# Eight row-split dk stores in place of five in a one-core attention forward and backward kernel

## The chip, the core and the metric

The kernel runs on one core of a Trainium2 chip. The core has a matrix engine (TensorE, PE in the profile), a vector engine (VectorE, DVE), a scalar engine (ScalarE, ACT), a general engine (GpSimd, POOL) and a queue engine (SyncE, SP). Transfers between HBM and the on-chip memory (SBUF) are issued by SP, ACT or POOL and carried out by 16 DMA engines that all issuers share. The metric is the device time of one execution in microseconds, lower is better. The kernel before took 1267.52 us (median of three runs, 1266.84 to 1269.59).

## The reference

A decode attention with its gradients, for 2 x 32 = 64 heads, one query row per head, 8192 keys of 128 numbers, all in bf16:

```
scores = einsum("bhqd,bhkd->bhqk", q, k) * D**-0.5      # Sq = 1, Sk = 8192, D = 128
p      = softmax(scores)
out    = einsum("bhqk,bhkd->bhqd", p, v)
out, vjp = jax.vjp(forward, q, k, v);  dq, dk, dv = vjp(grad_out)
returns out, dq, dk, dv
```

The inputs k and v are 2 MiB per head each, and so are the outputs dk and dv: dv is the outer product of p and grad_out, dk that of the score gradient and q. Everything else is small. So the kernel reads 268 MB and writes 268 MB.

## The kernel before, in words

**Tiles.** A head's k is one SBUF tile of 128 partitions x 64 x 128 bf16: partition p holds 64 consecutive keys, 16 KB that also lie together in HBM. v is the same. There are 12 such tiles (`NTILE`), so six heads are in flight. dk and dv are written over k and v in place: `outer` (line 469) multiplies on VectorE a quarter of a tile at a time, and after the fourth quarter it issues the store of the whole tile. A "row" below is one partition's 16 KB of a store or load: a load or a whole-tile store is 128 rows.

**Stages.** The loop at line 506 takes one step per quarter tile, eight steps per head (four quarters of k, then four of v), and overlaps four heads. Each step transposes a quarter on TensorE (`transpose_chunk`, line 232), copies it out of PSUM on ScalarE (line 241, two PSUM buffers), forms scores of the previous quarter (`score_chunk`), and does softmax, sums and outer products of earlier heads. The order on every engine is the order of the text (`pin`).

**Queues.** Loads go out on SP (`load`, line 106). The load of head i+6 reuses the tile of head i, so SP waits until that tile's store has landed everywhere. Whole-tile stores go out on POOL (line 493); those of the last head go out on SP in quarters. Every DMA is signalled by a semaphore; SP and ACT issues share one set of eight in rotation, POOL has another eight. A new DMA on a semaphore first waits for the landing of the previous one on it.

**The special stores.** `SPREAD` (line 23) names heads 6, 17, 28, 39 and 50. Their dk is not stored as 128 rows in one DMA, but by `by_rows` (line 96) in four: rows 8 to 127 (120 rows) with a cap on the descriptor (`cut`), then rows 0-2, 3-5 and 6-7 without. `turn(0)` (line 88) puts POOL's choice of DMA engine back to its start; `turn(n)` moves it on by issuing a tiny copy of n rows of 16 bytes into a scratch tile. `BACK` (line 26) asks, five steps after each special store, for `turn(0)` and `turn(5)`. At the start, five rows of q are loaded in the same way (line 129), which brings the choice to 5 for the first special store. The other 59 rows of q and the 64 rows of grad_out are loaded by SP (line 135).

Of the kernel before, what the change touches and what calls it, by code (L numbers as in the profile page):

```python
# [19 lines left out]
SW = 32  # L20
NTILE = 12
FIRST = 5
SPREAD = {
    i: ((8, 128, True), (0, 3, False), (3, 6, False), (6, 8, False)) for i in range(6, 56, 11)
}
BACK = {i + 1: FIRST for i in SPREAD}

@with_exitstack
def kernel(  # L30
# [11 lines left out]
    nc = tc.nc  # L42
    B, H, Sq, D = q.shape
# [5 lines left out]
    NT = Sk // P  # L49
# [6 lines left out]
    store_eng = nc.gpsimd  # L56
    pin = tc.keep_in_program_order
# [30 lines left out]
    def turn(n):  # L88

        if n:  # L90
            parts = turns.pop()
            pin(store_eng.dma_start(out=parts[:n, :], in_=q_rows[:n, : 2 * QT], max_dma_last_dim=2 * QT))
        else:
            pin(store_eng.inc_swdge_sem([], [], mode="reset_dge_cursor"))

    def by_rows(dst, src, steps):

        for step in steps:
            if len(step) == 1:
                turn(*step)  # L100
                continue
            p0, p1, cut = step
            cap = {"max_dma_last_dim": NT * D} if cut else {}
            pin(store_eng.dma_start(out=dst[p0:p1], in_=src[p0:p1], **cap))

    def load(i, w, pieces=(NCH,)):
        h = heads[i]
        t = kvp.tile([P, NT, D], BF16, tag=f"kv{slot_of(i, w)}", name="kvt")
        h.tile[w] = t
        src = (v_v if w else k_v)[i]  # L110
        c = 0
        for m in pieces:
            n0, n1 = c * CH, (c + m) * CH
            pin(load_eng.dma_start(out=t[:, n0:n1, :], in_=src[:, n0:n1, :]))
            c += m
# [1 line left out]
    load(0, 0, (1, 1, 2))  # L117

    q_rows = q.rearrange("b h s d -> (b h s) d")
    NTURN = len(BACK) + sum(len(step) == 1 and step[0] > 0 for x in SPREAD.values() for step in x)  # L120
    parts_all = const.tile([CH, NTURN, 2 * QT], BF16, name="parts_all")
    turns = [parts_all[:, n, :] for n in range(NTURN)]

    qd_nat = evp.tile([P, CH, P], BF16, tag="ev", name="qd_nat")
    for w, a in enumerate((q, grad_out)):
        rows = a.rearrange("b h s d -> (b h s) d")
        r0 = FIRST if w == 0 else 0
        if r0:
# [3 lines left out]
                    out=qd_nat[:r0, w, :], in_=rows[:r0], max_dma_last_dim=D  # L132
# [28 lines left out]
    for g in range(SG):  # L161
        nc.vector.tensor_copy(
            out=sel4[g * SW : (g + 1) * SW, :, g // 2, :],
            in_=ident_f[g * SW : (g + 1) * SW, g * SW : g * SW + 2 * NCH].rearrange(
                "p (c t) -> p c t", t=2
            ),
# [9 lines left out]
    for w in range(2):  # L176
        nc.vector.tensor_copy(
            out=qd_pair[:BH, w],
            in_=qd_nat[:BH, w, :]
# [33 lines left out]
    def window(i, w):  # L213

        pin(nc.scalar.copy(out=qwin[:, w, :, Q0 : Q0 + 2], in_=qpair[:, w, i]))
# [253 lines left out]
    def outer(i, w, c, ends):  # L469

        h = heads[i]
        n0 = c * CH
        shape = [P, CH, D // 2, 2]
        pin(
            nc.vector.tensor_tensor(  # L475
                out=h.tile[w][:, n0 : n0 + CH, :].rearrange("p n (e t) -> p n e t", t=2),
                in0=h.qb[w][:]
                .rearrange("p (e t) -> p e t", t=2)
                .unsqueeze(1)
                .to_broadcast(shape),  # L480
                in1=h.pair[w][:, n0 : n0 + CH, :].unsqueeze(2).to_broadcast(shape),
                op=ALU.mult,
            )
        )
        if c + 1 in ends:
            at = ends.index(c + 1)
            b0, b1 = (ends[at - 1] if at else 0) * CH, (c + 1) * CH
            dst = (dv_v if w else dk_v)[i]
            if w == 0 and i in SPREAD:
                by_rows(dst, h.tile[w], SPREAD[i])  # L490
            else:
                eng = load_eng if len(ends) > 1 else store_eng
                pin(eng.dma_start(out=dst[:, b0:b1, :], in_=h.tile[w][:, b0:b1, :]))  # L493
# [12 lines left out]
    for g in range(SL * BH + O0 + NCH + 4 - SL):  # L506
        now = [(g // SL - b, g % SL + b * SL) for b in range(4)]
        now = [(i, r) for i, r in now if 0 <= i < BH]

        def at(r0):  # L510

            return next((i for i, r in now if r == r0), None)

        def within(r0):

            return next(((i, r - r0) for i, r in now if r0 <= r < r0 + NCH), None)

        if (i := at(O1 + NCH)) is not None and i + AHEAD < BH:
            load(i + AHEAD, 0)
        if (i := at(O0 + NCH)) is not None and i + AHEAD < BH:  # L520
            load(i + AHEAD, 1)
        if x := within(O1):
            outer(x[0], 1, x[1], last if x[0] == BH - 1 else whole)
        if (i := at(O1 + NCH)) in BACK:
            turn(0)
            turn(BACK[i])
        if x := within(O0):
            outer(x[0], 0, x[1], last if x[0] == BH - 1 else whole)
        ev = None
        if g < SL * BH:  # L530
            i, r = divmod(g, SL)
            if r == NCH:
                begin(i)
                broadcast(i, 1)
            if r == NCH + 2:
                broadcast(i, 0)
            ev = transpose_chunk(i, r)
        if (i := at(A1 + NCH + 2)) is not None:
            join(i, 1)
        if (i := at(A0 + NCH + 2)) is not None:  # L540
            join(i, 0)
        if x := within(A1):
            acc(x[0], 1, x[1])
        if x := within(A0):
            acc(x[0], 0, x[1])
        if (i := at(NCH + 1)) is not None:
            spread_rows(i, 0)
        if (i := at(SL + 1)) is not None:
            spread_rows(i, 1)
        if (i := at(NCH + 3)) is not None:  # L550
            max_spread(i)
            expo(i)
        if prev is not None:
            score_chunk(*prev)
        prev = (g // SL, g % SL, ev) if ev is not None else None
        if (i := at(NCH + 1)) is not None and i + 1 < BH:
            window(i + 1, 0)
        if (i := at(1)) is not None and i > 0:
            window(i, 1)

        if (i := at(NCH)) is not None:
            keep_raw(i)
        if (i := at(SL)) is not None:
            keep_raw(i)
        if (i := at(NCH + 1)) is not None:
            max_part(i)
        if (i := at(NCH + 2)) is not None:
            max_all(i)
        if (i := at(NCH + 4)) is not None:
            normalise_p(i)  # L570
        if (i := at(SL + 1)) is not None:
            weigh(i)
        if (i := at(SL + 2)) is not None:
            normalise_ds(i)
        if (i := at(A1 + NCH)) is not None:
            pick(i, 1)
        if (i := at(A0 + NCH)) is not None:
            pick(i, 0)
# [37 lines left out]
```

## Time and profile before

| what | value |
|---|---|
| time, median of three runs | 1267.52 us (1266.84 to 1269.59) |
| the profiled execution's own time | 1267.85 us |
| its span, first to last instruction | 1266.1 us |
| TensorE busy | 1187.7 us, 94% |
| VectorE, ScalarE, GpSimd busy | 1031.3, 557.2, 80.6 us |
| bytes read from and written to HBM | 268.47 and 268.47 MB, 424 GB/s over the span |
| granted TensorE clock, mean | 0.988 |

The page gives for each engine the busy time, then 40 equal slices of the span in which each digit is a busy share in tenths. The line DMA is the mean busy share of the 16 DMA engines. "Issue to landing" is the time from a DMA's issue until its last part has arrived. The trace also holds one record per DMA packet (start, length, queue, bytes), but no number of the DMA engine that moved it. Queue q0 is POOL's, q1 is SP's; q8 and q14 carry the engines' instructions. All times inside the run are counted from the span's start.

### The profile page before, as it was taken

To read this page: it belongs to the slowest core of one execution; us is meant where nothing else is said; L and a number is where in the kernel's file an instruction comes from. 1 tells how busy PE (TensorE), PEld (TensorE's weight loads), DVE (VectorE), ACT (ScalarE), POOL (GpSimd) and SP (SyncE) were. 2 spreads that over 40 slices of the span, in tenths; PEclk is the share of its full clock that TensorE was granted. 3 is DMA by queue.
4 is the path that set the end of the run, shared out by engine and by line. 5 is a ranking of instruction groups with operands and counts; after the bars stand their busy time and mean duration, and the time that the engine had idled before them with its cause. 6 is when DMAs were issued, how large, how long until landed. Compare 5 with 4: busy or idle time off the path is not lost.

```text
span 1266.1 us, 24581 instructions
## 1 busy us (share of the span) xinstructions
PE 1187.7 (94%) x10056; PEld 783.1 (62%) x10056; DVE 1031.3 (81%) x2267; ACT 557.2 (44%) x769; POOL 80.6 (6%) x153
## 2 busy tenths in 40 slices
PE   6999999999999999999999999999999999999981
PEld 4666666666666666666666666666666666666650
DVE  3888888888888888888888888888888888887883
ACT  3444444444444444444444444444444444444430
POOL 0000010000010000001000001000000001000000
PEclk9999999999999999999999999999999999999995
DMA  9999999999999999999999999999999999999998
GB/s 393 422 429 429 429 428 429 429 429 429 430 429 428 429 429 429 429 429 429 423 428 430 430 429 428 428 427 430 429 430 428 429 429 427 429 429 429 429 430 336
DMA packets 39741, 538.53 MB, mean 425 GB/s; under 512 B 5236, under 2 KB 5236, under 8 KB 6516
## 3 DMA queue, kind: packets, MB, share of 16 engines
q1 hardware_dynamic: 20172, 272.70, 50.6%
q0 software_dynamic: 19456, 264.25, 49.1%
q8 instruction: 79, 1.29, 0.4%
q14 instruction: 34, 0.28, 0.1%
HBM read 268.47 MB, written 268.47 MB: 424 GB/s over the span
## 4 chain that ended last, share of the span: by engine, by line
PE 68%; DVE 16%; DMA 7%; another core or an unknown queue 4%; issue 2%; ACT 0%; SPq 0%; POOL 0%; ACTq 0%; DVEq 0%
PE tp L239 29%; PE acc L420 17%; PE raw L260 11%; DVE kvt L475 6%; PE sw L280 4%; DMA out_dram<-kvt 4%; DVE sel L443 4%; DVE rows L273 3%; DMA kvt<-in_v_dram 3%; PE sw L366 3%; PE sw L221 2%; PE sw L304 1%; DVE sel L437 1%; PE acc L457 1%
## 5 line engine op out<-in xcount | busy, mean ns | idle before, releaser
L241 ACT COPY ev<-tp 128x1024 f32<-128x1024 f32 x512 | 518.7, 1013 | 660.3 <-PE tp L239 654.8
L475 DVE TENSOR_TENSOR kvt<-qb,pair 128x2048 bf16<-128x2048 bf16 x512 | 617.2, 1216 | 0.2
L239 PE MATMUL tp<-ident_f,kvt 128*128 128x128 f32 x4096 | 547.6, 277 | 3.1 <-DMA kvt<-in_v_dram 2.6
L239 PEld LDWEIGHTS tp<-ident_f,kvt 128*128 128x128 f32 x4096 | 454.0, 144 | 84.2 <-issue 64.6
L260 PE MATMUL raw<-ev,qwin 128*32 128x512 bf16 x2048 | 209.5, 399 | 0.0
L420 PE MATMUL acc<-kvt,dS_pad 128*64 128x512 bf16 x1024 | 160.7, 395 | 0.8 <-DVE dS_pad L406 0.8
L420 PE MATMUL acc<-kvt,E_pad 128*64 128x512 bf16 x1024 | 159.5, 391 | 0.6 <-DVE E_pad L331 0.6
L280 PEld LDWEIGHTS sw<-sel,rows 128*128 128x128 f32 x1024 | 123.9, 191 | 52.4 <-DVE sel L443 25.9
L443 DVE SCALAR_TENSOR_TENSOR sel<-acc,diag,sel 128x128 f32<-128x128 f32 x384 | 134.7, 351 | 13.6
L260 PEld LDWEIGHTS <-qwin 128*32 128x32 bf16 x2048 | 52.7, 93 | 135.4 <-issue 131.0
L280 PE MATMUL sw<-sel,rows 128*128 128x16 f32 x1024 | 136.3, 265 | 0.0
L493 POOL DMA_DIRECT2D out_dram<-kvt x121 | 64.6, 533 | 1062.3 <-DVE kvt L475 484.4
L273 DVE COPY rows<-raw 128x512 f32<-128x512 f32 x128 | 88.6, 692 | 47.0 <-PE raw L260 47.0
L299 DVE TENSOR_REDUCE st<-sw 1x1 f32<-1x128 f32 x64 | 17.8, 278 | 55.9 <-PE sw L298 55.9
L221 PE MATMUL sw<-ident_f,qT 128*128 128x128 bf16 x128 | 28.9, 226 | 36.2 <-DVE st L294 36.2
L420 PEld LDWEIGHTS <-dS_pad 128*64 128x64 bf16 x1024 | 36.6, 108 | 34.9 <-issue 31.8
L366 PEld LDWEIGHTS sw<-st,ones 128*128 128x128 f32 x256 | 37.9, 186 | 31.0 <-issue 15.3
L420 PEld LDWEIGHTS <-E_pad 128*64 128x64 bf16 x1024 | 36.0, 108 | 33.6 <-issue 31.5
L366 PE MATMUL sw<-st,ones 128*128 128x1 f32 x256 | 48.8, 260 | 0.5 <-DVE st L337 0.5
L437 DVE TENSOR_SCALAR sel<-acc,diag 128x128 f32<-128x128 f32 x128 | 43.8, 342 | 0.0
L457 PEld LDWEIGHTS acc<-ones,sel 128*128 128x128 f32 x256 | 39.0, 193 | 7.2 <-DVE sel L443 7.2
L457 PE MATMUL acc<-ones,sel 128*128 128x1 f32 x256 | 36.7, 212 | 6.1 <-DVE sel L443 6.1
(54 smaller groups left out, 381.3 us busy)
## 6 DMA issues: line engine op xcount, KB each, us to landing
out_dram<-kvt POOLq DMA_DIRECT2D x121, 2048.0 KB, 44.9
kvt<-in_v_dram SPq DMA_DIRECT2D x64, 2048.0 KB, 20.1
kvt<-in_k_dram SPq DMA_DIRECT2D x63, 2048.0 KB, 20.2
out_dram<-kvt POOLq DMA_DIRECT2D x5, 1920.0 KB, 49.5
out_dram<-kvt SPq DMA_DIRECT2D x8, 512.0 KB, 20.1
kvt<-in_k_dram SPq DMA_DIRECT2D x2, 512.0 KB, 4.4
kvt<-in_k_dram SPq DMA_DIRECT2D x1, 1024.0 KB, 6.9
out_dram<-kvt POOLq DMA_DIRECT2D x10, 48.0 KB, 49.1
```

The source lines that it names most:

```text
L239: pin(nc.tensor.transpose(tp[:, m, :], two, ident_f[:]))
L241: pin(nc.scalar.copy(out=ev[:], in_=tp[:]))
L260: nc.tensor.matmul(h.raw[g * SW : (g + 1) * SW, :], lhsT=qwin[:, w, e, q0 : q0 + SW], rhs=cols[:, b, :, e], start=(c == 0), stop=(c == NCH ...
L273: pin(nc.vector.tensor_copy(out=h.rows[:], in_=h.raw[:]))
L280: nc.tensor.matmul(h.score[w].rearrange("p (n m t) -> p n m t", m=QT, t=2)[:, :, m, :], lhsT=h.rows[:, m * P : (m + 1) * P], rhs=sel4[:].r ...
L366: nc.tensor.matmul(out, lhsT=ones[:].to_broadcast([P, P]), rhs=col, start=True, stop=True)
L420: nc.tensor.matmul(h.acc[w][g : g + CW, :], lhsT=wts[:, n0 : n0 + CW], rhs=rows[:, n0 : n0 + QT, :].rearrange("p n d -> p (n d)"), start=( ...
L437: nc.vector.tensor_scalar(out=h.sel[:], in0=block, scalar1=diag[:, 0:1], scalar2=None, op0=ALU.mult)
L443: nc.vector.scalar_tensor_tensor(out=h.sel[:], in0=block, scalar=diag[:, b : b + 1], in1=h.sel[:], op0=ALU.mult, op1=ALU.add,)
L457: nc.tensor.matmul(h.acc[w][:, 0:1], lhsT=h.sel[:], rhs=ones[:], start=True, stop=True)
L475: nc.vector.tensor_tensor(out=h.tile[w][:, n0 : n0 + CH, :].rearrange("p n (e t) -> p n e t", t=2), in0=h.qb[w][:] .rearrange("p (e t) -> ...
L493: pin(eng.dma_start(out=dst[:, b0:b1, :], in_=h.tile[w][:, b0:b1, :]))
```

## The change

Eight heads instead of five have a special dk store. At heads 6, 15, 24 and 32 it is the same split as before (120 rows, then 3, 3 and 2). At heads 40, 47, 51 and 55 the large piece has 104 rows; at 40 the other 24 rows follow in one piece, at 47, 51 and 55 a piece of 17 capped rows after a `turn` of 11 or 15, and a last piece of 7 rows. The pieces without the cap (the small rows) are no longer issued by POOL: `by_rows` keeps them in a list, and ScalarE issues them at the start of the next step. `BACK` now holds the turns for each head: reset and 5 after the first three, and 2, 12, 4 and 14 without a reset after the next four.

```diff
+SMALL = ((0, 3, False), (3, 6, False), (6, 8, False))
 SPREAD = {
-    i: ((8, 128, True), (0, 3, False), (3, 6, False), (6, 8, False)) for i in range(6, 56, 11)
+    6: ((8, 128, True),) + SMALL,
+    15: ((8, 128, True),) + SMALL,
+    24: ((8, 128, True),) + SMALL,
+    32: ((8, 128, True),) + SMALL,
+    40: ((24, 128, True), (0, 24, False)),
+    47: ((0, 104, True), (11,), (104, 121, True), (121, 128, False)),
+    51: ((0, 104, True), (15,), (104, 121, True), (121, 128, False)),
+    55: ((24, 128, True), (11,), (0, 17, True), (17, 24, False)),
 }
-BACK = {i + 1: FIRST for i in SPREAD}
+BACK = {7: (0, 5), 16: (0, 5), 25: (0, 5), 33: (2,), 41: (12,), 48: (4,), 52: (14,)}
...
+    pending = []
+
     def by_rows(dst, src, steps):
...
             p0, p1, cut = step
-            cap = {"max_dma_last_dim": NT * D} if cut else {}
-            pin(store_eng.dma_start(out=dst[p0:p1], in_=src[p0:p1], **cap))
+            if cut:
+                pin(store_eng.dma_start(out=dst[p0:p1], in_=src[p0:p1], max_dma_last_dim=NT * D))
+            else:
+                pending.append((dst[p0:p1], src[p0:p1]))
...
-    NTURN = len(BACK) + sum(len(step) == 1 and step[0] > 0 for x in SPREAD.values() for step in x)
+    NTURN = sum(n > 0 for x in BACK.values() for n in x) + sum(
+        len(step) == 1 and step[0] > 0 for x in SPREAD.values() for step in x
+    )
...
+        for dst, src in pending:
+            pin(nc.scalar.dma_start(out=dst, in_=src))
+        pending.clear()
...
         if (i := at(O1 + NCH)) in BACK:
-            turn(0)
-            turn(BACK[i])
+            for n in BACK[i]:
+                turn(n)
```

## The prediction

> **What bounds the kernel now.** I read the page from the top: engines, DMA line, queues, DMA issues. Then the busy time by stretches, SP's waits, SP's last issues, and the DMA view of the last 20 us.
>
> ```profile
> span 1266.1 us, 24581 instructions
> ...
> PE 1187.7 (94%) x10056; PEld 783.1 (62%) x10056; DVE 1031.3 (81%) x2267; ACT 557.2 (44%) x769; POOL 80.6 (6%) x153
> ...
> DMA  9999999999999999999999999999999999999998
> ...
> q1 hardware_dynamic: 20172, 272.70, 50.6%
> q0 software_dynamic: 19456, 264.25, 49.1%
> q8 instruction: 79, 1.29, 0.4%
> q14 instruction: 34, 0.28, 0.1%
> ...
> out_dram<-kvt POOLq DMA_DIRECT2D x121, 2048.0 KB, 44.9
> kvt<-in_v_dram SPq DMA_DIRECT2D x64, 2048.0 KB, 20.1
> ...
> out_dram<-kvt POOLq DMA_DIRECT2D x5, 1920.0 KB, 49.5
> ...
> out_dram<-kvt POOLq DMA_DIRECT2D x10, 48.0 KB, 49.1
> ```
>
> TensorE looks as busy as the DMA engines, but the DMA line is full from the first slice on. The stretches (us, then the four busy times, POOL's, clock, DMA share, GB/s):
>
> ```profile
> 740.00:1060.00 320.00, 310.26 (x2645) 204.90 (x2642) 269.46 (x590) 146.53 (x203) 21.38 (x39) 1.00 1.01 429
> ...
> 1220.00:1250.00 30.00, 18.18 (x124) 9.94 (x122) 23.62 (x50) 4.05 (x6) 0.54 (x2) 0.74 1.01 428
> 1250.00:1266.00 16.00, 0.00 (x0) 0.00 (x0) 0.00 (x0) 0.00 (x0) 0.00 (x0) 0.50 0.61 251
> ```
>
> The DMA share is 1.01 until 1250 us, while computing has ended by then. SP's waits and last issues, and the DMA digits from 1246 to 1266 us (0.5 us each):
>
> ```profile
> SPq L114 <- DMA out_dram<-kvt: 1124.7, 119, 27.5
> ```
>
> ```profile
> 1238.31 7.07 SPq L493 DMA_DIRECT2D out_dram<-kvt  x5
> 1247.34 3.54 SPq L585 DMA_DIRECT2D out_dram<-nat  x2
> ```
>
> ```profile
> DMA  9999999979977977978696786866666542100000
> ```
>
> SP spends 1124.7 us waiting to reload a tile whose store has not landed: loads follow stores, not computing. The last store is issued at 1250.4 us, so the last 14 us are only backlog, and the digits fall early: some DMA engines finish long before others. Hence the end is the work of the slowest of 16 engines, and what the change moves between them is all that counts.
>
> **Which engine ends when.** On a busy engine a packet starts 3 or 4 ns before the recorded end of the one before (611 ns for 16 KB, so 607 ns a row; 6 ns for a 4-byte packet). Strung together like this, the packet records of 100 to 1265 us fall into 16 chains with almost no gap. Every whole-tile DMA shows there as 8 rows and a 4-byte semaphore write. Marks name some chains: the five-row turns put a 16-byte packet on five (engines 0 to 4); one of these five gets no row of the 120-row stores (engine 4), only fillers; rows 0-2, 3-5 and 6-7 always fall on the same three of the five (engines 0, 1, 2: 3, 3, 2 rows). SP's 59 rows of q (a prime) all lie on one of these three.
>
> - engine 0: 15 extra rows over five stores; ends at 1259.4 us
> - engine 1: 15 extra rows, an 8 KB instruction fetch every 122 us (as many as ScalarE would need); 1264.5, the last
> - engine 2: 10 extra rows; 1256.8
> - engine 3: a fetch every 66 us, at 0.6 us each; 1263.8
> - engine 4: 40 rows fewer, but 628 instead of 612 ns a row; 1259.3
> - eight of engines 5 to 15: in strict rotation the 16 KB fetches of q8, 9 to 10 each, 1.33 us each; 1261.6 to 1263.2
> - the other three: no fetch, no extra row; work done by 1250.5 to 1251.3
>
> Their mean is 1259.9 (from the last stretch: 1250 + 0.61 x 16 = 1259.8), so perfect balance would save 4.6 us, 0.36%. 1.6 us pass from the last packet to the span's end and 1.75 from there to the profiled time, 1267.85, which is 0.33 above the median.
>
> **The change part by part.** *Rows.* A capped piece goes in equal shares to the largest number of engines up to 16 that divides its rows (120 rows: 15 with 8; the prime 59: one), starting where the last capped piece stopped (after 5: engine 5 on, 4 left out). So 104 rows take 13 engines, 17 one. Counting on: after head 32 the place is 4, the turn of 2 makes it 6, head 40 leaves out 3 to 5; 12 makes 15, head 47 leaves out 12 to 14, and 11 puts the 17 rows on engine 7; 4 makes 12, head 51 leaves out 9 to 11, 15 puts 17 on engine 8; 14 makes 7, head 55 leaves out 4 to 6, 11 puts 17 on 15. Uncapped rows start at engine 0: 24 give 2 each to 0-11, 7 one each to 0-6. After minus before, in rows: engines 0, 1: 17 - 15 = +2; 2: +3; 3: -3; 4: -3; 5: -11; 6: -3; 7, 8: +19; 9-11: -6; 12-14: -8; 15: +17 (sum 0).
>
> At 0.607 us a row: engine 1 gains 1.2 us; +19 is 11.5 us, which the three idle engines have; engine 3 falls to 1262.0, 9 to 14 to 1258 or 1259.
>
> *Fillers.* A left-out engine gets a 4-byte filler per packet of a taking one (16 on engine 4 per store). A 17-row piece is 34 half-row packets, so 34 x 6 ns on every other engine, three times: 0.6 us. Eleven turns instead of six: 0.1 us.
>
> *Small rows on ScalarE.* 16 issues of 0.33 us (as SP's) on an engine busy 44%; POOL loses 15 of 0.5 us, at 6% busy. Both cost nothing while the backlog lasts; without it they would sit in ScalarE's copies, for which TensorE's transposes wait. The new instructions and their waits, some 40 against a fetch of 128, bring engine 1 0 or 0.6 us of fetching; I take 0.2.
>
> *Waits added.* A small store waits for VectorE's last outer product (1.2 us) and for the previous DMA on its semaphore. In the changed order that is a load still under way: by the landings of before, ScalarE would wait at head 32 for the v of head 35 (lands 665.5, ScalarE there at 655.6): 9.9 us; at 55 7.2, at 51 5.0, at 6 3.5, at 24 3.0, at 47 1.1. Queued behind are the copies, then TensorE. Bounds for the end: 0 to 9.9 us (not their sum: each wait leaves computing later relative to loads, which shortens the next). But computing runs ahead of DMA by 0.8 us a head (a load landed 16.2 us before use at head 36, 1.8 at head 54), so before, its lead was spent by head 56. Of 9.9 us, 7 heads of 0.8 leave at most 4 at the end, which 12 us of backlog hide: 0. Without that backlog it would be 4. SP and POOL: their DMAs wait for one five to eight places back; loads land in 20.1 us and come every 9.8, so that is past; POOL's special issues wait for fewer semaphores than before (74.9 us of such waits, all hidden).
>
> *Sum.* Engine 1: 1264.5 + 1.2 + 0.7 + 0.2 = 1266.6; the next, 7 or 8: 1251.2 + 11.5 + 0.5 = 1263.2. With 1.6 + 1.75 after it: 1269.95 against 1267.85, **+2.1 us; from the median 1269.6 us**, +0.16%. A measurement of this kernel tells about 0.2% (2.5 us) from no change.
>
> [...] One chain is slow by 16 ns a row, and it is engine 4's, the one that the 120-row stores pass over; the chains of 5 to 15 run at 611 to 612 ns, fetches apart. [...]
>
> **The rivals.**
>
> 1. *The loaded engines are not the idle ones (slower).* The records do not number engines 5 to 15. For the match: the trace has eight with fetches and three without, the change takes rows from exactly eight of the eleven (5, 6, 9-14) and loads three; against: nothing else ties them. If one of 7, 8, 15 carries fetches, it ends at 1262.6 + 11.5 + 0.5 = 1274.6, time 1277.6. It decides once a loaded engine's old end is over 1255. Chance 0.13.
> 2. *The 17-row piece is shared out* (two rows each on engines 0 to 7, one on 8, as 17 = 8 x 2 + 1, if the cap is not what chooses). Engine 1 gets 6 rows more, 3.6 us, and fillers fall to nearly none: 1272.6. For: the uncapped pieces begin at 0; against: every capped piece ran in equal shares. Chance 0.08.
> 3. *ScalarE's waits become the path.* Computing would have to end over 12 us later; with the longest wait twice, 20 us, less 12: 8 us, 1275.5. Against: each shortens the next. Chance 0.05.
> 4. *Engine 1 is relieved* (ScalarE's small rows start elsewhere, or the last chain is one of the eight). Then engines 7 and 8 end last at 1263.2: -1.3 us, 1266.2. For: no ScalarE store is in the trace; against: SP's uncapped 59 rows went to one of engines 0 to 2. Chance 0.14.
>
> **How the numbers follow.** My forecast has 0.60, own range 1267.5 to 1271.0 (fetch, fillers, the spread of the runs). It is within 0.2% (up to 1270.05) for 0.37, slower for 0.22, faster for 0.01. Rival 4 adds 0.11 to the same and 0.03 to faster, rivals 1 and 2 0.21 to slower, rival 3 0.03 to slower and 0.02 to the same. So faster 0.04, same 0.50, slower 0.46. Eight in ten: from rival 4's end with the runs' spread, 1265.5, to past rival 2, 1275.0; rival 1 stays out.
>
> **What would show it.** The DMA digits of the last 16 us should fall later and more steeply, with the last packet at about 1266.6. The three early chains should end near 1262 to 1263; the last should be the one with ScalarE's fetches. At head 32 ScalarE should show a wait of several us for a load, and the loads' lead should still shrink to near 0. A chain that ends beyond 1270 alone means rival 1 or 2; a full DMA line with computing beyond 1260, rival 3. Any idle DMA time before 1240 us would make the whole sum wrong.

## The result, and the profile after

The changed kernel took 1281.31 us (median of six runs, 1279.62 to 1287.74) against 1267.65 us (six runs, 1266.84 to 1269.59) for the kernel before: a ratio of 1.0113, 95% interval 1.009 to 1.0135. That is 13.7 us slower, where 2.1 us were forecast and 1275.0 was the upper end of the range. The profiled execution took 1282.98 us.

From the page of the changed kernel: the span, the engines, three of the forty-slice rows, the queues (packets, MB, share of 16 engines) and some DMA issues.

```profile
span 1281.2 us, 24594 instructions
...
PE 1190.4 (93%) x10056; PEld 784.7 (61%) x10056; DVE 1031.6 (81%) x2267; ACT 557.3 (43%) x769; POOL 79.8 (6%) x146
...
PE   6999999999999999999969999999999999999991
...
DMA  9999999999999999999999999999999999999996
GB/s 391 424 430 430 427 430 428 429 429 428 428 428 431 429 428 430 424 428 430 427 431 424 423 431 427 425 418 427 428 424 424 412 399 411 415 410 416 428 430 282
...
q1 hardware_dynamic: 20172, 272.70, 50.0%
q0 software_dynamic: 21200, 263.00, 48.9%
q10 hardware_dynamic: 142, 1.26, 0.4%
...
out_dram<-kvt POOLq DMA_DIRECT2D x118, 2048.0 KB, 45.3
out_dram<-kvt POOLq DMA_DIRECT2D x4, 1920.0 KB, 43.2
out_dram<-kvt POOLq DMA_DIRECT2D x4, 1664.0 KB, 61.1
```

The engines' busy times are those of before within 3 us, so the work has not grown. The DMA row is as full as before. What has changed is the row under it: the DMA engines are just as busy, but in slices 32 to 37 (993 to 1185 us) they move 399 to 416 GB/s, where most slices have 424 to 431. The same by stretches:

```profile
740.00:1060.00 320.00, 310.84 (x2646) 205.22 (x2645) 269.96 (x591) 146.68 (x204) 22.81 (x39) 1.00 1.01 421
1060.00:1220.00 160.00, 151.67 (x1291) 100.26 (x1292) 131.86 (x287) 70.45 (x97) 11.53 (x20) 1.00 1.01 417
1220.00:1250.00 30.00, 27.03 (x209) 16.00 (x208) 25.41 (x58) 10.00 (x14) 1.60 (x3) 0.93 1.01 428
1250.00:1282.00 32.00, 3.73 (x16) 1.80 (x14) 8.48 (x17) 0.00 (x0) 0.00 (x0) 0.50 0.65 272
```

The last three columns are the granted clock, the DMA share and GB/s. The second of these stretches in the kernel before:

```profile
1060.00:1220.00 160.00, 152.34 (x1288) 99.96 (x1287) 131.57 (x287) 70.88 (x98) 10.62 (x20) 1.00 1.01 429
```

The same DMA share of 1.01 with 417 in place of 429 GB/s means that packets take longer; a busy engine is not an engine at its rate. ScalarE's and SP's waits, and the DMA row from 1262 to 1282 us (0.5 us a digit):

```profile
ACT ev L255 <- PE tp L253: 644.4, 503, 2.6
ACT ev L255 <- DMA out_dram<-kvt: 13.1, 1, 13.1
```

```profile
SPq L126 <- DMA out_dram<-kvt: 1136.6, 116, 27.8
```

```profile
DMA  7989988899676765553442311110000000000000
```

ScalarE stands once for long, 13.1 us at head 32. SP still spends nearly all its time waiting for stores to land. The last digits show an end that is later, and flatter than in the kernel before.

**Where the time is, packet by packet.** Strung into 16 chains as for the prediction, the packet records confirm the allotment of rows: 120 rows on 15 engines, 104 on 13, 17 on one, ScalarE's 24 on twelve and its 7 on seven. The three chains with a 17-row piece are the ones without TensorE's fetches. The chain that ends last is, as forecast, the one with ScalarE's fetches (engine 1). But it ends at 1279.3 us in place of 1266.6, and every other chain is late as well.

What grew is the length of packets. "Lengthening" below is the time of packets of 16, 8 and 4 KB beyond 611, 309 and 159 ns, where that is over 60 ns, summed over all 16 engines from 100 us on. It is 49 us in the kernel before and 210 us in the changed one: (210 - 49) / 16 = 10.1 us more for each engine. With the 2.1 us of the prediction's sum that makes 12.2 of the 15.1 us between the two profiled executions (1282.98 against 1267.85). On average over the 16 engines the account closes. The prediction's own check of the mean end, 1250 + 0.61 x 16 = 1259.8 us, now reads 1250 + 0.65 x 32 = 1270.8, which is 11.0 us later; rows that move between engines add nothing to a mean, fillers and turns add 0.7 by the prediction and the lengthening 10.1. What is left is engine 1's own: it ends 8.5 us behind the mean where it was 4.7 us behind, and its two rows more are 1.2 of these 3.8 us.

The lengthening lies around the special stores (the table takes 12 us to either side). "Share spread" is the time from the first to the last 8 KB packet of a store's capped rows, which travel as halves, so it tells how far apart the engines are by then:

| kernel | head | share spread, us | lengthening, us |
|---|---|---|---|
| before | 6, 17, 28, 39, 50 | 15, 17, 25, 31, 36 | 1.3, 1.3, 7.7, 3.3, 3.8 |
| after | 6, 15, 24, 32 | 15, 19, 26, 37 | 1.8, 2.5, 6.5, 12.6 |
| after | 40, 47, 51, 55 | 41, 43, 50, 46 | 21.6, 32.1, 58.3, 35.6 |

Two of the expectations below put the kernel before lower, at 8 us in all or at 0 to 3.5 us a store; the text goes by the measure of this table.

38 us of the changed kernel's lengthening are in the 77 rows that ScalarE issues. Those of its 2- and 3-row pieces take 611 ns but for three (up to 1102), the 24 of head 40 up to 1941; those of the seven-row pieces took, in order of start:

```
head 47   611 1995  611 1031 2660 2102 2484 ns
head 51  4118 4582 2954 3504 2891 1745 1552 ns
head 55  2073 3326 2858  611 2168  621 1847 ns
```

### The profile page after: what moved, and what is told of

The parts are those of the page before. It is cut to its first block, busy times and chain, and to the rows that moved or that the text cites. A ratio compares the mean times of both kernels' runs of the same rounds, so it can differ in the third digit from the quotient of the medians.

```text
span 1281.2 us, 24594 instructions
## 1 busy us (share of the span) xinstructions
PE 1190.4 (93%) x10056; PEld 784.7 (61%) x10056; DVE 1031.6 (81%) x2267; ACT 557.3 (43%) x769; POOL 79.8 (6%) x146
## 4 chain that ended last, share of the span: by engine, by line
PE 56%; issue 17%; DVE 13%; DMA 10%; another core or an unknown queue 1%; POOL 1%; ACT 0%; SPq 0%; POOLq 0%; DVEq 0%; ACTq 0%
PE tp L253 24%; PE acc L434 14%; PE raw L274 9%; DVE kvt L489 5%; DMA kvt<-in_v_dram 5%; PE sw L294 4%; DMA out_dram<-kvt 3%; DVE sel L457 3%; DVE rows L287 2%; PE sw L380 2%; DMA kvt<-in_k_dram 2%; PE sw L235 1%; PE sw L318 1%; DVE sel L451 1%
```

## The experiments

Theory A was that engines which read rows of the same few partitions at one time slow each other, and that ScalarE's own queue, being empty, brings them together. Theory B was the prediction's third rival: ScalarE's wait delays computing, and that the end. Theory C was that ScalarE's queue is served slowly.

### 1. The small rows back on POOL

```diff
             else:
-                pending.append((dst[p0:p1], src[p0:p1]))
+                pin(store_eng.dma_start(out=dst[p0:p1], in_=src[p0:p1]))
```

> The changed kernel with its small rows issued by POOL at once, as the kernel before does, in place of ScalarE; the eight special stores, their rows and turns stay. Theory A (several engines that read rows of the same few partitions at one time slow each other, and the third queue of ScalarE brings them together): the 38 us of lengthening on ScalarE's packets mostly vanish, engine 1 ends about 5 us earlier or somewhat less, 1275 to 1278 us; the stores of heads 47, 51 and 55 still show 16 KB packets of about 1.2 us. Theory B (ScalarE's wait of 12.9 us at head 32 delays computing and with it the end): with no ScalarE store there is no such wait, and the time is 1268 to 1270 us, with the late packets at 0.61 us. Theory C (ScalarE's queue is itself served slowly): the lengthening goes with the queue, 1270 to 1275 us.

Measured: 1276.51 us, ratio to before 1.0062 (1.0042 to 1.0082). One of the four executions, of 2807.68 us, counts in that median; the other three took 1273.54 to 1277.87 us, their median is 1275.16. The lengthening fell from 210 to 103 us; at the heads of the changed kernel it is 1.4, 1.6, 3.9, 5.2, 9.7, 11.3, 24.7 and 16.6 us. So 5 to 6 us by the medians (6.5 by the ratios) go with ScalarE issuing, and theory B alone is out: without any ScalarE store the kernel is still 6 to 8 us slower than the 1268.72 us of the kernel before beside it. By stretches, the GB/s of the changed kernel (421 and 417) come part of the way back:

```profile
740.00:1060.00 320.00, 310.29 (x2645) 205.06 (x2643) 269.70 (x589) 145.91 (x203) 23.93 (x41) 1.00 1.01 427
1060.00:1220.00 160.00, 150.84 (x1264) 99.15 (x1260) 128.65 (x282) 69.92 (x97) 12.53 (x22) 0.98 1.01 422
```

### 2. The five stores of before, small rows by ScalarE

```diff
-SPREAD = {
-    6: ((8, 128, True),) + SMALL,
...
-    55: ((24, 128, True), (11,), (0, 17, True), (17, 24, False)),
-}
-BACK = {7: (0, 5), 16: (0, 5), 25: (0, 5), 33: (2,), 41: (12,), 48: (4,), 52: (14,)}
+SPREAD = {i: ((8, 128, True),) + SMALL for i in range(6, 56, 11)}
+BACK = {i + 1: (0, FIRST) for i in SPREAD}
```

> The five special stores of the kernel before (heads 6, 17, 28, 39 and 50, 120 rows without engine 4 and then 3, 3 and 2 rows), with the small rows issued by ScalarE, as in the changed kernel. Theory A: nothing here lets seven or more engines read the same few partitions at once, so packets lengthen by less than 15 us in the sum over 16 engines (8 in the kernel before, 162 more in the changed one over the whole run), and the time is 1266.5 to 1268.7 us, though ScalarE waits for several us at some head. Theory B: ScalarE waits about as long as in the changed kernel, and the time is 1276 to 1280 us. Theory C: the 15 small DMAs of 2 or 3 rows show packets of over 1 us, and the time is 1268 to 1271 us.

Measured: 1273.0 us, 1.0034 (1.0021 to 1.0047), a miss for all three. ScalarE's 40 row packets took 611 ns each, which removes theory C. The lengthening is 76 us, 1.7 us an engine above before. The rest shows in the stretches and ScalarE's waits:

```profile
ACT ev L246 <- DMA kvt<-in_v_dram: 23.6, 3, 11.5
```

```profile
1060.00:1220.00 160.00, 155.43 (x1326) 102.38 (x1323) 135.16 (x296) 73.46 (x101) 8.76 (x17) 1.00 1.01 427
1220.00:1250.00 30.00, 28.27 (x240) 18.47 (x240) 25.15 (x56) 12.29 (x18) 1.89 (x4) 1.00 0.88 372
1250.00:1272.00 22.00, 8.94 (x37) 3.94 (x36) 14.48 (x30) 0.00 (x0) 0.00 (x0) 0.52 0.72 290
```

Here the DMA share is 0.88 between 1220 and 1250 us, and TensorE works until 1265.6 us (1247.1 before). The last store is issued at 1267.0 instead of 1250.9. So this kernel did turn into the third rival: with ScalarE waiting late (9.1 us at head 50) the lead is not won back, and the DMA engines run dry at the end. The mechanism is real; it is not what bounds the changed kernel, whose DMA row stays full with computing over at 1259.4 us.

### 3. and 4. No 17-row piece, with ScalarE and with POOL

```diff
-    47: ((0, 104, True), (11,), (104, 121, True), (121, 128, False)),
-    51: ((0, 104, True), (15,), (104, 121, True), (121, 128, False)),
-    55: ((24, 128, True), (11,), (0, 17, True), (17, 24, False)),
+    47: ((0, 104, True), (104, 128, False)),
+    51: ((0, 104, True), (104, 128, False)),
+    55: ((24, 128, True), (0, 24, False)),
 }
-BACK = {7: (0, 5), 16: (0, 5), 25: (0, 5), 33: (2,), 41: (12,), 48: (4,), 52: (14,)}
+BACK = {7: (0, 5), 16: (0, 5), 25: (0, 5), 33: (2,), 41: (12,), 52: (14,)}
```

> The changed kernel with heads 47, 51 and 55 stored as 104 rows plus 24 rows by ScalarE, like head 40: no piece of 17 rows on one engine, no seven rows after it. By the count of rows engine 1 then has 5 rows more than in the kernel before (3 us). Theory A (place of the rows): the windows of the three late stores lengthen packets by about 18 us each, as that of head 40 did, in place of 26 to 49 us; engine 1 ends about 4 us earlier than in the changed kernel, 1273 to 1277 us. Theory B (ScalarE's wait at head 32, which stays): 1280 to 1282 us. A third, that the 17 rows on one engine alone are at fault: 1270.5 to 1272 us, the count of rows.

> The fourth corner of a square: as the third experiment (heads 47, 51 and 55 as 104 rows plus 24, no 17-row piece), but with the small rows issued by POOL at once. The other corners: 17-row pieces with ScalarE 1281 us, 17-row pieces with POOL 1276.5, none with ScalarE 1285.7. Theory A1 (ScalarE's own queue is what makes many engines read the same few partitions at one time, since it is empty and is served at once on all of them): the lengthening in the late windows falls from 35 to about 10 us each, engine 1 has its 5 rows more, 1271 to 1275 us. Theory A2 (a store that leaves out three engines, and so gives every engine other partitions than its neighbour stores, is itself the cause): as slow as with ScalarE, 1280 to 1285 us. If it comes out above the 17-row corner with POOL (1276.5) by more than the 3 us of rows, the 17-row pieces are no cost but a help.

Measured: with ScalarE 1285.72 us, 1.015 (1.0099 to 1.02), lengthening 228 us; with POOL 1275.3 us, 1.0055 (1.0037 to 1.0073), lengthening 102 us. The 17-row pieces are not at fault, since taking them out leaves POOL's corner as it was (1275.3 against 1275.16 or 1276.51) and ScalarE's no better. ScalarE's issuing costs 5 to 6 us with 17-row pieces and 10 without them, by the medians. POOL's corner came out just above the 1271 to 1275 us of theory A1. My expectation for ScalarE's corner (1273 to 1277) missed: 24 rows by ScalarE lengthen as much as 17 and 7 do, and computing ends only at 1271.6 us there, with ScalarE waits of 12.6 and 10.2 us.

### 5. Only the late small rows on POOL

```diff
+        late = not steps[0][0] == 8
...
+            elif late:
+                pin(store_eng.dma_start(out=dst[p0:p1], in_=src[p0:p1]))
             else:
                 pending.append((dst[p0:p1], src[p0:p1]))
```

> The changed kernel with the small rows of heads 40, 47, 51 and 55 (24, 7, 7 and 7 rows) issued by POOL at once; those of heads 6, 15, 24 and 32 (3, 3 and 2 rows) stay with ScalarE, and with them its wait of some 10 us at head 32. Between the changed kernel (1281.3 us) and the one with all small rows on POOL (1276.5). If the 38 us of lengthened ScalarE packets, all at the late heads, are what ScalarE costs: 1276 to 1278 us. If ScalarE's waits cost it (computing later, and DMA idle at the end, as in the run with five stores by ScalarE): 1280 to 1282 us.

Measured: 1276.0 us, 1.0068 (1.0049 to 1.0088), the same as with all rows on POOL, although ScalarE's wait is still there:

```profile
ACT ev L259 <- DMA out_dram<-kvt: 11.9, 1, 11.9
```

So the wait at head 32 costs nothing, as the prediction said, and what ScalarE costs is the late pieces of 24 and 7 rows.

### 6. and 7. Which rows are slow to read together

Both are the kernel before plus scratch stores by ScalarE.

```diff
+                if w == 0 and i in PROBE:
+                    n, kind = PROBE[i]
+                    rows = {"n": slice(121, 128), "h": slice(0, 28, 4), "f": slice(121, 128), "s": slice(0, 121, 20)}[kind]
+                    to = slice(0, 112, 16) if kind == "f" else slice(0, 7)
+                    probes.append((scratch[n][to], h.tile[w].rearrange("p n d -> p (n d)")[rows]))
...
+        for dst, src in probes:
+            pin(nc.scalar.dma_start(out=dst, in_=src))
+        probes.clear()
```

> The kernel before with eleven extra stores of seven 16 KB rows by ScalarE into a scratch tensor that nothing reads (extra work: 77 rows, 1.2 MB, some 3 to 6 us of time, which is not the point). Their packets are: kind n (heads 13, 25, 37) seven neighbouring partitions, 121 to 127, to seven neighbouring rows of HBM; kind f (19, 31, 43) the same partitions to rows 16 apart in HBM; kind h (16, 40) partitions 0, 4 to 24 to neighbouring rows; kind s (22, 34, 46) partitions 0, 20 to 120, far apart, to neighbouring rows. Theory A (reading the same few partitions is what slows): n and f take 1.5 to 4.5 us a packet, s 0.61 to 1.2 us, h between or as s. If neighbouring rows of HBM are what slows: f, and not s, is 0.61 us. Theory C (the queue): all kinds take over 1.2 us alike.

> The kernel before with 21 extra stores by ScalarE into scratch that nothing reads (extra work, 147 rows, 2.4 MB; its time is not the point). Seven kinds, each three times (early, middle, late): 2, 3 or 4 neighbouring partitions from 121 on; 7 neighbours from 0 on; 7 that are 2 apart; 7 that are 3 apart; 16 neighbours from 0 on. If neighbours share one path that one or two engines fill, then 2 neighbours take up to 0.61 x 2 = 1.2 us a packet, 3 up to 1.8, 4 up to 2.4, 7 up to 4.3 wherever they lie, and 2 or 3 apart in proportion to how many fall on one path (4 apart was 0.61 us in the second half of the first batch). If only the last partitions are slow, 7 from 0 on are 0.61 us.

Measured, 16 KB packets in ns:

| rows read at once | packets | median | longest | over 700 |
|---|---|---|---|---|
| 121 to 127, to neighbouring HBM rows | 21 | 1249 | 3180 | 16 |
| 121 to 127, to HBM rows 16 apart | 21 | 2372 | 5493 | 18 |
| 0, 4, ... 24 | 14 | 611 | 634 | 0 |
| 0, 20, ... 120 | 21 | 611 | 636 | 0 |
| 2 from 121 on | 6 | 958 | 2475 | 3 |
| 3 from 121 on | 9 | 1834 | 3288 | 8 |
| 4 from 121 on | 12 | 611 | 2304 | 5 |
| 0 to 6 | 21 | 1376 | 4796 | 15 |
| 7 that are 2 apart | 21 | 639 | 2082 | 8 |
| 7 that are 3 apart | 21 | 611 | 1380 | 6 |
| 0 to 15 | 48 | 825 | 3238 | 27 |

Five of the first probe's windows show it in GB/s at a full DMA share (kinds, in order: neighbours, 4 apart, neighbours with HBM rows apart, 20 apart, neighbours):

```profile
297.00:302.00 5.00, 5.00 (x46) 3.26 (x46) 4.57 (x11) 2.03 (x2) 0.00 (x0) 1.00 1.02 410
355.00:360.00 5.00, 5.00 (x47) 3.17 (x44) 4.58 (x11) 2.19 (x3) 0.00 (x0) 1.00 1.02 436
411.00:416.00 5.00, 5.00 (x46) 3.26 (x47) 4.57 (x12) 2.03 (x2) 0.53 (x1) 1.00 1.01 395
469.00:474.00 5.00, 5.00 (x47) 3.22 (x45) 4.58 (x11) 2.14 (x3) 0.00 (x0) 1.00 0.99 419
526.00:531.00 5.00, 5.00 (x47) 3.25 (x45) 4.57 (x11) 2.11 (x3) 0.00 (x0) 1.00 1.00 377
```

Spreading the HBM rows did not help, and spreading the partitions removed the lengthening altogether, on the same queue. So it is the partitions: the 35 packets 4 or 20 apart took 611 to 636 ns, those of seven neighbours mostly over 0.7 us, wherever they lie (0 to 6 as well as 121 to 127). The dose is not a simple count, though. Of two neighbours one took 2339 ns in the middle probe and 2475 in the late one, more than twice 611, and both 611 or 612 in the early one; one set of four took 611 ns throughout. Other readers of the same partitions may count too; no run separates them. Nor did a run show why rows 4 or 20 apart go free where neighbours do not.

### 8. Lag made by hand

```diff
+                if w == 0 and i == 15:
+                    rows = h.tile[w].rearrange("p n d -> p (n d)")[:17]
+                    for n in range(3):
+                        pin(store_eng.dma_start(out=scratch[n], in_=rows, max_dma_last_dim=NT * D))
+                    turn(0)
+                    turn(FIRST)
```

> The kernel before with three extra stores of 17 rows (extra work into scratch that nothing reads) at head 15, each on one engine: engines 5, 6 and 7 have 10.3 us more to do than their neighbours from there on and lag by it. The special stores themselves stay as they are; in the kernel before their packets are lengthened by 0, 0, 3.5, 1.7 and 1.3 us (summed over the engines) at heads 6, 17, 28, 39 and 50. By counting rows alone engine 5 or 6 ends last, at 1262 to 1263 + 10.4, and the time is 1275.5 to 1277 us. Lag theory (a special store gives each engine partitions that the whole-tile stores give to other engines; while some engines are still in the whole-tile store before it or already in the one after it, too many read the same few partitions): the lengthening stays 0 at head 6, and is over 8 us at each of heads 17, 28, 39 and 50. If the lengthening comes from the form of the store or from its head alone, it stays at 0 to 5 us everywhere.

Measured: 1292.16 us in its one run, far beyond the count. The three extra pieces read the same 17 partitions on three engines at once, and around them the lengthening is 86 us by itself, some of it in loads; that runs into the window of head 17 (37 us), which says nothing then. Of the other three windows, head 28 has 10.9 us, 39 has 4.2 and 50 has 9.9, where more than 8 was expected at each. Three engines behind the others raise the lengthening only a little; the experiment does not decide.

### 9. and 10. The price of a row, without a new form of store

```diff
-    i: ((8, 128, True), (0, 3, False), (3, 6, False), (6, 8, False)) for i in range(6, 56, 11)
+    i: ((8, 128, True), (0, 2, False), (2, 4, False), (4, 6, False), (6, 8, False)) for i in range(6, 56, 11)
```

```diff
-    i: ((8, 128, True), (0, 3, False), (3, 6, False), (6, 8, False)) for i in range(6, 56, 11)
+    i: ((8, 128, True), (0, 3, False), (3, 6, False), (6, 7, False), (7, 8, False)) for i in range(6, 56, 11)
```

> The kernel before with the eight small rows of each special store as 2, 2, 2 and 2 in place of 3, 3 and 2, by POOL: engines 0 and 1 get one row more per special store, 5 in all, engine 2 two fewer. This tests the price of a row on engine 1 without any new form of store: counting rows, engine 1 ends 3.0 us later and the time is 1270.7 to 1271.2 us (+0.24%). If engine 1 isn't the one that bounds the kernel before, 1267.5 to 1268.5 us.

> The kernel before with the eight small rows as 3, 3, 1 and 1, by POOL: engine 1 gets one row less per special store (5 in all, -3.0 us), engine 2 one less, engine 0 two more... that is 5 more rows than the 15 of before on engine 0, which ends at 1259.4 + 3.0 = 1262.4. Engine 1 ends at 1261.5, and engine 3, untouched at 1263.8, is last: -0.7 us, 1267.2 us. If it is slower than before, rows are not what decides.

Measured: 5 rows more on engine 1 give 1271.23 us, 1.0024 (1.0013 to 1.0034), as counted. 5 rows less give 1267.41 us, 0.9996 (0.9987 to 1.0005); the 0.7 us that were counted there can't be told from no change. So counting rows fits as long as the stores keep their form, but not cleanly: in its profiled execution (1272.54 us) the first of the two has 97 us of lengthening against 49, which is 3.0 us an engine, and count and lengthening together make 6.0 us where 4.7 were measured.

### 11. Another plan: three 17-row pieces in mid-run

```diff
     6: ((8, 128, True),) + SMALL,
...
+    17: ((0, 105, True), (3,), (105, 122, True), (122, 125, False), (125, 128, False)),
+    28: ((0, 105, True), (4,), (105, 122, True), (122, 125, False), (125, 128, False)),
+    39: ((0, 105, True), (11,), (105, 122, True), (122, 125, False), (125, 128, False)),
+    50: ((8, 128, True),) + SMALL,
 }
...
+BACK = {i + 1: (0, FIRST) for i in SPREAD}
```

> Another plan of five special stores, all small rows by POOL: heads 6 and 50 as in the kernel before (120 rows without engine 4, then 3, 3 and 2 rows); heads 17, 28 and 39 as 105 rows (7 each on 15 engines, without engine 4), 17 rows on the one engine 7, 8 or 15, and 3 and 3 rows on engines 0 to 2. Rows against the kernel before: engines 0 and 1 -6, 2 -3, 3 -3, 4 as before, 5, 6 and 9 to 14 -3, the three idle ones +14. At 0.607 us a row the last engine ends at 1262.0 us in place of 1264.5: by the count of rows alone 1266.2 us against 1268.7, -0.2%. If the three 105-row stores lengthen packets as the late stores of the first experiment did (12 us each over 16 engines, 2.3 us an engine in all) 1268.5 us, no change; if engines that read each other's partitions at a lag cost more than that, 1270 us or more.

Measured: 1271.57 us (1268.16 to 1274.05), 1.0027 (1.0016 to 1.0038): slower, though rows promised 0.2% and the lengthening is small (62 us). By the packets' time in the last 20 us its DMA engines end at 1261.7 us on average (1259.8 before), the last one at 1266.5. Strung back from its end, that last chain carries no instruction fetch after 1030 us, so it is neither engine 1 nor engine 3 nor one of the eight with TensorE's. Which of the others it is was not established, so why this plan fails stays open.

### 12. and 13. Form, drift or distance

Small rows by POOL in both; the first replaces the five stores of the kernel before, the second turns the order of experiment 4 round.

```diff
+SPREAD = {i: ((1,), (24, 128, True), (0, 24, False)) for i in range(6, 56, 11)}
+BACK = {i + 1: (0, FIRST) for i in SPREAD}
```

```diff
+    6: ((1,), (24, 128, True), (0, 24, False)),
+    13: ((0, 104, True), (104, 128, False)),
+    17: ((0, 104, True), (104, 128, False)),
+    21: ((24, 128, True), (0, 24, False)),
+    28: ((8, 128, True),) + SMALL,
+    36: ((8, 128, True),) + SMALL,
+    45: ((8, 128, True),) + SMALL,
+    55: ((8, 128, True),) + SMALL,
 }
...
+BACK = {7: (12,), 18: (14,), 22: (0, 5), 29: (0, 5), 37: (0, 5), 46: (0, 5)}
```

> The kernel before with its five special stores in another form, at the same heads 6, 17, 28, 39 and 50: 104 rows on 13 engines (3, 4 and 5 left out) and 24 rows, by POOL, in place of 120, 3, 3 and 2. Lengthening of packets around each special store, summed over the engines: 1.3, 1.3, 7.7, 3.3 and 3.8 us in the kernel before, and 9.9, 15.7, 18.3 and 15.3 us for this form at heads 40, 47, 51 and 55 of the experiment without 17-row pieces by POOL. If the form of the store is the cause: 10 to 18 us at each of the five heads. If it is how far the engines have drifted apart by then: 1 to 2 us at heads 6 and 17, rising to over 10 at heads 39 and 50. If it is stores that follow each other by only 4 to 7 heads: under 8 us at each. By counting rows engines 6 to 11 get 10 rows more and the last of them ends at 1263.2 + 6.1: 1272.6 us, plus the lengthening.

> The experiment without 17-row pieces by POOL (1275.3 us) with the order of its eight special stores turned round: the four stores of 104 and 24 rows at heads 6, 13, 17 and 21 (again 7, 4 and 4 heads apart), the four of 120, 3, 3 and 2 rows at heads 28, 36, 45 and 55. The same rows on the same engines in sum: counting rows, engine 1 ends 3 us later than in the kernel before, 1271 us. If how far the engines have drifted apart is the cause, the four early stores lengthen packets by 1 to 4 us each in place of 10 to 18, and the time is 1270.5 to 1273 us. If the form of the store or the short distance between them is the cause, the early stores show 10 to 18 us each and the time stays at 1274 to 1277 us.

Measured: the spaced one 1278.43 us in its one run, the early one 1283.65 us, 1.0114 (1.008 to 1.0147). Around each special store:

| kernel | form | heads | share spread, us | lengthening, us |
|---|---|---|---|---|
| spaced | 104 + 24 | 6, 17, 28, 39, 50 | 16, 21, 31, 40, 48 | 7.9, 7.4, 15.2, 9.1, 26.1 |
| early | 104 + 24 | 6, 13, 17, 21 | 16, 20, 31, 37 | 6.2, 7.2, 36.3, 17.3 |
| early | 120 + 3 + 3 + 2 | 28, 36, 45, 55 | 41, 40, 38, 42 | 26.9, 25.6, 18.1, 17.4 |

The distance alone is out: at 11 heads apart there are still 26 us at head 50. The form counts: 6 to 8 us at a spread of 16 us, where 120 rows have 1.3 to 1.8. The time of the run is not what matters: early stores that follow each other let the engines drift at once (31 us of spread by head 17), and they lengthen at once. And the old form of 120 rows, which in the kernel before cost 3 to 8 us at spreads of 25 to 36, costs 17 to 27 at about 40. My expectation of small early lengthening failed because I had put drift down to time; the uneven stores make it.

Over the 78 special stores of the twelve kernels in which all is computed and nothing is added, lengthening goes with spread: 2.5 us on average for spreads up to 20 us (21 stores), 8.5 for 21 to 30 (16), 12.0 for 31 to 36 (14), 23.9 beyond (27). Single stores stray far from these means: in experiment 9 two stores of 120 rows lengthened by 22 and 24 us at spreads of 29 and 34. Longer packets also widen the spread, so this alone does not say which comes first.

### 14. and 15. Twelve stores left out, for less drift

```diff
+LEFT = (41, 42, 43, 44, 45, 46, 48, 49, 50, 52, 53, 54)
...
-            else:
+            elif not (w == 1 and i in LEFT):
                 eng = load_eng if len(ends) > 1 else store_eng
```

> The first experiment (the eight special stores with their 17-row pieces, every row issued by POOL) with twelve stores of dv left out, those of heads 41 to 46, 48 to 50 and 52 to 54: the DMA engines then run out of work before heads 47, 51 and 55, and those that are behind catch up. Its output lacks these twelve stores, and its time (some 50 us less) is not the point. Lengthening around the special stores was 9.7, 11.3, 24.7 and 16.6 us at heads 40, 47, 51 and 55, with 35 to 41 us from the first to the last engine's share of a store. If drift between the engines is the cause: head 40 as before, and at 47, 51 and 55 less than 8 us each, with the store's share spread over less than 25 us. If the form or the short distance is the cause: 10 to 20 us each as before, however closely the engines run.

> The changed kernel with the same twelve stores of dv left out (its output lacks them). ScalarE's packets of 16 KB: in the changed kernel the seven rows of heads 47, 51 and 55 took 1.6, 3.0 and 1.9 us each on average. If it is that seven engines read seven neighbouring partitions at once, they stay at 1 to 3 us even when the engines run in step; the rest of the lengthening (POOL's packets) falls as in the run with POOL alone. If ScalarE's packets are slow only because the engines have drifted apart, they are 0.61 to 0.8 us.

Measured, at heads 47, 51 and 55 (lengthening of POOL's packets alone, since with stores left out loads lengthened by 13 to 26 us per window, against 2 to 5):

| kernel | share spread, us | POOL's packets, us | ScalarE's packets, mean ns |
|---|---|---|---|
| first experiment | 38, 41, 40 | 8.8, 19.7, 14.4 | |
| the same, stores left out | 31, 30, 31 | 1.4, 8.0, 12.5 | |
| changed kernel | 43, 50, 46 | 22.0, 37.3, 32.9 | 1642, 3049, 1929 |
| the same, stores left out | 26, 24, 28 | 6.1, 7.4, 15.9 | 1056, 752, 643 |

The engines did not come fully into step (the spread stayed at 30 us with POOL alone, where less than 25 was expected), as the loads ran ahead into the gap and kept the DMA row at nine until head 47. The lengthening of POOL's packets fell with the spread in every window, to between a fifth and a half in the changed kernel, but at head 55 it stayed at 12.5 and 15.9. For ScalarE's rows neither expectation held. At head 55 seven engines read partitions 17 to 23 between 1109.29 and 1110.53 us, six of them at one time, and six of the seven packets took 611 to 616 ns (the seventh 827): 7 x 16 KB in 1.24 us, 92 GB/s. So six neighbours at once are not slow by themselves. What this experiment thinned out is the other stores under way that read there as well; that these make the difference is the likely reading, not a shown one.

## Why the prediction was wrong

- **DMA bounds the kernel, and its slowest engine the end: right.** The DMA row is full until the last store, SP waits for stores, and the last chain is engine 1's. No DMA idle time appeared before 1240 us, which I had named as the sign of a wrong sum; that sign cannot see longer packets. The GB/s row can.
- **The rows per engine and their price: right.** All allotments are in the packet records, and experiment 9 gives the time that the count gives, though with some lengthening beside it; experiment 10's 0.7 us are too little to tell. Rival 2 (a 17-row piece shared out) did not occur.
- **"At 0.607 us a row" for every row of the changed kernel: this is the step that failed.** It took the packet length of a run whose special stores lengthen packets by 17 us in all, and gave it to stores of another form, place and issuer. Those lengthen by 171 us. Over the whole run the lengthening grew from 49 to 210 us, 10.1 us an engine: the largest term of the result, and the sum put it at nothing.
- **"Both cost nothing", of the small rows on ScalarE: wrong in its size.** I priced the issue time and the wait, and both are indeed hidden (experiment 5). Experiments 1 and 5 against the changed kernel put the cost of moving the late pieces to ScalarE at 5 to 6 us.
- **Waits added: right here.** 9.9 us were forecast at head 32. ScalarE issued its three stores there at 655.8, 659.1 and 668.7 us, so the wait forecast took 9.4 us and another of 3.0 us stood ahead of it. The waits at the other heads were shorter than forecast, 2.5 us at most. Computing ended at 1259.4 us, the last store was issued at 1263.3, and the backlog went on to about 1280. In experiment 2 the same kind of wait, later in the run, did become the path. The backlog of 12 us that I counted on is no constant: a late wait uses it up.
- **Rival 1 (loaded engines are not the idle ones; 1277.6) came nearest to the time and is wrong as a cause, so that its nearness is luck.** The three loaded chains have no fetches, and they end at 1275.7, 1274.1 and 1269.5 us, all before engine 1. Nor is any of them slow by the record: over their last 70 us and more, the median of their 16 KB packets is 611 ns.
- **Rival 4 (engine 1 relieved): wrong.** Engine 1 stayed last.

The counts and the lengthening together, for the profiled runs against the one of before (1267.85 us), lengthening beyond before's 49 us and divided by 16:

| kernel | rows counted | lengthening | sum | measured |
|---|---|---|---|---|
| after | 2.1 | 10.1 | 12.2 | 15.1 |
| small rows on POOL | 2.1 | 3.4 | 5.5 | 5.7 |
| no 17 rows, POOL | 3.0 | 3.3 | 6.3 | 7.5 |
| no 17 rows, ScalarE | 3.0 | 11.2 | 14.2 | 17.7 |
| late small rows on POOL | 2.1 | 4.2 | 6.3 | 8.6 |
| 2, 2, 2 and 2 | 3.0 | 3.0 | 6.0 | 4.7 |
| 3, 3, 1 and 1 | -0.7 | 1.1 | 0.4 | 1.1 |
| three 17-row pieces | -2.5 | 0.8 | -1.7 | 2.0 |
| spaced | 4.7 | 3.1 | 7.8 | 10.6 |
| early | 3.0 | 8.5 | 11.5 | 15.2 |

The rest, -1.3 to +3.7 us and above zero in all but one, has the size to be expected if lengthening falls unevenly on the engines, but that was not shown. Experiment 2 is not in the table, since computing became the path there; in the fourth line computing is late as well.

**What stays open.** Shown: packets are longer by 10.1 us an engine; those that ScalarE issues lengthen by the partitions that they read; ScalarE's late pieces cost 5 to 6 us, the form adds a little, and the lengthening goes with the engines' drift, which uneven stores bring about early or late. Not shown: that POOL's packets lengthen for the same reason as ScalarE's in the probes, and that drift is the cause of it rather than its companion. The lag made by hand and the drained runs point the same way, but neither reached its own expectation in every window.

## What to carry to other kernels

When all DMA engines are busy and the end is the slowest one's work, count the rows that are moved, but do not take the length of a packet as fixed: here it grew when engines were given other partitions than in the whole-tile stores. Before doing that, look at what neighbouring stores read at the same time; that this is the cause is likely here and not shown. Read GB/s beside the DMA share: a full share with 417 in place of 429 GB/s is where 10 us went. And a second issuing queue is not only a matter of issue cost: here its rows were served at once and together. ScalarE's seven rows of a late head started 3.5 to 4.9 us after their issue and within 1.4 us of each other, where POOL's had landed only 52 us after theirs (first experiment).

## What the runs showed of the hardware

- Reads of 16 KB rows from seven neighbouring partitions took up to 5.5 us instead of 0.61, to neighbouring HBM rows as well as to rows 16 apart; from partitions 4 or 20 apart, to neighbouring HBM rows, they took at most 0.64.
- Seven rows from partitions 17 to 23 at head 55 took 0.61 to 3.33 us in the changed kernel, and 0.61 us but for one of 0.83 with twelve other stores left out.
- With stores left out, loads lengthened in turn: 22 to 26 us around the late special stores of the drained run by POOL, against 2 to 5 in the one that keeps its stores.
- A 17-row capped piece goes to one engine and 104 rows to 13, as 8 KB halves; TensorE's 16 KB fetches (79 in all, one every 15.5 us) rotate strictly over eight engines, here those numbered 5, 6 and 9 to 14 by the rows that they were given.
